# A fused transformer backward pass: kv and W' blocks between query halves, gate-gradient stores moved to GpSimd, two tails as column tiles

## The chip, the cores and the metric

The kernel runs on one core of a Trainium2 chip. The metric is the device time in microseconds of one execution, the median of several runs. A profile of one execution names its span, from the first instruction to the last. TensorE multiplies matrices out of SBUF into PSUM, VectorE (DVE), ScalarE (ACT) and GpSimd (POOL) work on elements, SyncE (SP) issues transfers; ScalarE and GpSimd issue some too. Each engine runs its own instructions in program order and waits on semaphores for the others.

## The reference

A block of a transformer, forward and backward: linear attention with 32 heads, then a gated MLP, each behind a layer norm and with a residual. Outputs are the block's result and the gradients of the input and of the five weight matrices. S = 2048 rows, D = 640, F = 1728, bf16.

```python
h  = x + A(layernorm(x));  h2 = h + B(layernorm(h))

def A(x):                       # wqkv: D x 3D, wo: D x D, 32 heads of 20
    q, k, v = heads(x @ wqkv)
    phi = lambda t: where(t > 0, t + 1, exp(t)) + 1e-6
    pq, pk = phi(q), phi(k)
    kv = einsum("bhsd,bhse->bhde", pk, v);  z = pk.sum over s
    o = (pq @ kv) / (pq . z + 1e-6)
    return o @ wo

def B(x):
    return (silu(x @ w1) * (x @ w3)) @ w2

out, vjp = jax.vjp(block, x, wqkv, wo, w1, w3, w2);  grads = vjp(grad_out)
```

## The kernel before, in words

Rows are worked in 16 tiles of 128 (`ST`), columns of D in five blocks of 128 (`DT`), the MLP in 14 chunks of 128 columns of F (`FT`; the last has only `FL` = 64) and four strips of 512 rows (`SC`). The order of the work is written out by hand: the Python program issues instructions one after another, and each engine's queue keeps that order. [...]named tiles rotate through a few buffers each, and a tile that is asked for again waits until the reader of its buffer's previous content is done.

The stages, with their times in the profile:

- 0 to 60 us: layer norm of x, the key projection with phi (`phi`, `phi_rest`), M = pk^T x (`m_part`, `m_end`), the sum z (`z_late`, `z_row`, which broadcasts it into `Zb`) and part of the query projection (`q_tile`). From 57 us on, `r_prod`, `r_red`, `r_inv`, `r_scale` make the normalised queries: a product with `Zb` on GpSimd, a sum per head, a reciprocal and a scaling on VectorE, and `r_T` transposes the result by DMA. `r_head(t)` is the last four of these for tile t.
- 60 to 90 us: the rest of M, the kv blocks (`kvT_block` and `f2_kv`, whose masked copy goes to `bd`), and W' = kv wo (`f2_wT`, which reads `bd` and is transposed into `Wp` by DMA). `q_late(t, between)` computes one query tile in two halves of 320 columns; `between` is put between the first and the second half. `run(...)` is the list in which all of these are put in order.
- 90 to 103 us: the attention output plus residual, tile by tile and half by half (`f2_half`, `f2_at`), its layer-norm statistics (`Stats.part`: VectorE, then a pow on GpSimd), the normalised `hn` (`f2_hn`) and its transpose by TensorE (`f2_ht` for the first four tiles). `mlp_ghh(n)` is chunk n of the MLP's upstream gradient g w2^T (`ghh_chunk`), some of which are computed here ahead of their use.
- 103 to 349 us: the MLP forward and the element-wise part of its backward, strip by strip and chunk by chunk (`mlp`, `mlp_pair`). `ghh` runs two chunks ahead. Two chunks make a pair; VectorE's seven products of a pair go out through `drain`, between other work. Results go to DRAM (`store`): `hh`, and the two halves of `gg_d`, the gate and the up gradients. `o2_steps` is the MLP's second product of the strip before, spread between chunks.
- 349 to 408 us: the w2 gradient (13 chunks of 128 rows of F, and a 64-row tail, `gw2_tail`).
- 408 to 571 us: the gradient of `hn`, the layer norm's backward, the attention's backward up to queries.
- 571 to 636 us: gradients of wqkv (`grad_halves`, called through `fill` as filler), the small D x D squares (`square`, `unload`: ScalarE copies 380 columns, then VectorE 260), transposes of `gkvT` (`trk`), and the key gradient per tile. The squares, `trk` and the key gradient share the three PSUM buffers `dkv`.
- 636 to 830 us: the gradient of x (`e_gxn`), then the gradients of w1 and w3 as 40 jobs of 432 columns (`grad_job`), each copied by ScalarE and stored.

The lines that the change moves most in `run` and in the MLP pair, before:

```python
(q_late, 10, f2_mT), (f2_kv, 2), (f2_kv, 3), (f2_kv, 4), (phi_rest,), (q_late, 11), (f2_wT, 0), (f2_wT, 1),
...
op(gate, gate, gh, to=gg_d, r0=F)          # store issued by SyncE
...
for i in range(DT):
    unload(square(wqT[:, 2 * DT:, :], gkvT, i), gm[:, i, :])
    if i > 0:
        fill(1)
```

Of the kernel before, what the change touches and what calls it, by code (L numbers as in the profile page):

```python
# [9 lines left out]
P = 128  # L10
# [45 lines left out]
def kernel(  # L56
# [73 lines left out]
    class Stats:  # L130
# [13 lines left out]
        def part(self, src, t, j):  # L144
            if j == 0:
                self.st[t] = cp.tile([P, 2, 6], F32, name="st6", bufs=4)
            V.bn_stats(out=self.st[t][:, j, :], in_=src[:, t, j * HD:(j + 1) * HD])
            if j == 0:
                return
            V.bn_aggr(out=self.mv[:, t, :], in_=self.st.pop(t)[:])  # L150
            V.tensor_scalar(out=self.ve[:, t:t + 1], in0=self.mv[:, t, 1:2], scalar1=EPS_LN, scalar2=None, op0=ALU.add)
            G.tensor_tensor(out=self.rs[:, t:t + 1], in0=self.ve[:, t:t + 1], in1=mhalf[:, 0:1], op=ALU.pow)

# [214 lines left out]
    def ghh_chunk(n, acc):  # L368

        c, fc = divmod(n, FT)  # L370
        mm5_to(acc, w2T, fc, g2T[c])
        if n % 2 == 0:
            ghh[n // 2] = pf.tile([P, 2, W], BF16, name="ghh", bufs=4)
        A.copy(out=ghh[n // 2][:, n % 2, :], in_=acc[:])  # L374
# [141 lines left out]
    m_part(2, range(8))  # L516
    z_row((0, 1), big())
    z_row((2, 3, 4), big())
# [3 lines left out]
    m_part(2, range(8, ST))  # L522
# [29 lines left out]
    r_head(5)  # L552
    r_prod(7)
# [167 lines left out]
    def mlp_pair(c, k, sig, s2, gate, up, gh):  # L721
# [14 lines left out]
        op(gate, gate, gh, to=gg_d, r0=F)  # L736
# [4 lines left out]
    def o2_steps(c, q=dma, tag="o2"):  # L741
# [4 lines left out]
        for n, (i, j, fc) in enumerate(jobs):  # L746
            if fc == 0:
                o2["ps"] = ps.tile([P, 512], F32, name="o2", tag=tag, bufs=2)
                if j == 0:
                    o2["sb"] = pf.tile([P, D], BF16, name="h2", bufs=2)  # L750
            T.matmul(o2["ps"][:, 0:HD], lhsT=hhT[c][:, fc, i * P:(i + 1) * P],  # L751
                     rhs=w2[:, fc, j * HD:(j + 1) * HD], start=(fc == 0), stop=(fc == FT - 1))
            if fc == FT - 1:
# [3 lines left out]
                if j == 1:  # L757
                    q(out=out0S[:, t, :], in_=o2["sb"][:])
# [17 lines left out]
    def run(*steps):  # L776
# [5 lines left out]
    run((q_late, 10, f2_mT), (f2_kv, 2), (f2_kv, 3), (f2_kv, 4), (phi_rest,), (q_late, 11), (f2_wT, 0), (f2_wT, 1),  # L782
        (phi_rest,), (q_late, 12), (f2_wT, 2), (f2_wT, 3), (phi_rest,), (q_late, 13, lambda: f2_wT(4)),
        (r_red, 6), (r_inv, 6), (r_scale, 6), (load_x, 2, 4), (r_T, 6), (q_late, 14), (load_x, 4, 8), (load_g2T, 1), (r_store, 4, 6),
        (mlp_ghh, 4), (q_late, 15),
        (sig_table,), (f2_half, 0, 0), (f2_half, 1, 0), (f2_half, 0, 1), (f2_half, 1, 1), (f2_hn, 0), (mlp_ghh, 5),
        (f2_half, 2, 0), (f2_hn, 1), (f2_m_out,), (load_w2T, 8 * P, 10 * P), (f2_half, 2, 1),
        (f2_ht, 0), (mlp_ghh, 6), (f2_half, 3, 0), (f2_hn, 2), (f2_w_out,), (f2_ht, 1), (f2_half, 3, 1), (phi_rest, 2),
        (q_out, 10, 14), (f2_ht, 2), (f2_hn, 3), (mlp_ghh, 7), (load_w2T, 10 * P, F), (f2_half, 4, 0), (f2_ht, 3),
        (f2_half, 4, 1), (r4_out,), (r_red, 7), (r_inv, 7), (r_scale, 7), (r_T, 7), (r_store, 6, 8), (q_out, 8, 10))  # L790
# [39 lines left out]
    for c in range(SC):  # L830
# [8 lines left out]
        for fc in range(FT):  # L839
# [17 lines left out]
            if fc == 3 and 0 < c < SC - 1:  # L857
# [59 lines left out]
    gt = ps.tile([P, DT, FL], F32, name="gt", tag="gw", bufs=4)  # L917

    def gw2_tail():

        for c in range(DT):
            for t in range(ST):
                T.matmul(gt[:, c, :], lhsT=g2[:, t, c * P:(c + 1) * P], rhs=hb[3][:, t, P:P + FL],  # L923
                         start=(c == 0 and t == 0), stop=(t == ST - 1), skip_group_check=True)
        sb = br.tile([P, DT, FL], BF16, name="gts")
        A.copy(out=sb[:], in_=gt[:])
        return sb

    def gw2_tail_out(sb):
        tr = ps.tile([P, DT, P], BF16, name="gttr", tag="gw", bufs=4)  # L930
        for c in range(DT):
            T.transpose(tr[:FL, c, :], sb[:, c, :], ident[:])
        ob = br.tile([P, D], BF16, name="gw2o", bufs=2)
        A.copy(out=ob[:FL].rearrange("p (c n) -> p c n", c=DT), in_=tr[:FL])
        A.dma_start(out=out_6[F - FL:F, :], in_=ob[:FL])

    for fc in range(FT - 1):
        b, i = divmod(fc, 4)
        if fc == FT - 2:
            sb = gw2_tail()  # L940
        acc = ps.tile([P, 2, 512], F32, name="gw", bufs=4)
        for j in range(2):
# [3 lines left out]
            if fc == FT - 2 and j == 0:  # L946
                gw2_tail_out(sb)
# [284 lines left out]

    fill(4)
# [8 lines left out]
    for i in range(DT):  # L1242
        unload(square(qp, kvN, i), dwoT[:, i, :])
        if i > 0:
            fill(1)
    dma(out=rows(dwoT_d), in_=dwoT[:])
    br.release()
# [7 lines left out]
    bo.release()  # L1255
    bv = pool("bv")
    pkT = bv.tile([P, DT, S], BF16, name="pkT")
    small = bv.tile([P, ST, D], BF16, name="small", tag="hnN")
    mN, gkv_b, gm = (small[:, n:n + DT] for n in (0, DT, 2 * DT))
    gzd = small[:, 3 * DT, :].rearrange("p (m q) -> p m q", q=P)  # L1260
# [4 lines left out]
    dma(out=mN, in_=m_v)  # L1265
# [3 lines left out]
    for i in range(DT):  # L1269
        unload(square(wqT[:, 2 * DT:, :], gkvT, i), gm[:, i, :])  # L1270
        if i > 0:
# [8 lines left out]
    for c, ms in SQ_BLOCKS:  # L1280
        tr = ps.tile([P, len(ms), P], BF16, name="trk", tag="dkv", bufs=3)
        for i, m in enumerate(ms):
            T.transpose(tr[:, i, :], gkvT[:, m, c * P:(c + 1) * P], ident[:])
        V.tensor_copy(out=gkv_b[:, c, ms[0] * P:(ms[-1] + 1) * P].rearrange("p (i q) -> p i q", q=P), in_=tr[:])

    for t in range(ST):
# [23 lines left out]
        if t == 1:  # L1310
            load_xnT(3)
        if t in (0, 4):
            load_wqT(t // 4)
# [110 lines left out]
```

## Time and profile before

| | |
|---|---|
| device time, median of 3 runs | 832.5 us (831.24 to 832.78) |
| span of the profiled execution | 830.0 us |
| TensorE busy | 818.9 us, 5540 matmuls |
| VectorE busy | 454.3 us |
| ScalarE busy | 319.4 us |
| GpSimd busy | 110.2 us |
| TensorE's share of the chain that ended last | 88% |
| moved by DMA | 157.59 MB, mean 190 GB/s |
| stores of `gg_d` from `gate` (SyncE) | 24 of 256 KB, median 3.4 us to landing |
| stores of `gg_d` from `ghh` (GpSimd) | 24 of 256 KB, median 3.4 us to landing |

Busy time is the time in which at least one instruction of the engine is in flight. Matmuls are pipelined, so a single one lasts longer than the distance to the next: what counts for TensorE is the distance from start to start. Idle time of an engine that is not the bottleneck costs nothing. The chain of waits follows the end of the kernel back through what released each step.

### The profile page before, as it was taken

Reading aid. Unit: us, or ns where it says so; the run is one execution under the profiler, and the core shown is the slowest. Engines: PE = TensorE matmul, PEld = TensorE weight load, DVE = VectorE, ACT = ScalarE, POOL = GpSimd, SP = SyncE. Lnnn points to the kernel's source line nnn. Section 1 sums busy time; section 2 is a strip of 40 time slices with the busy share of each in tenths; the row PEclk is TensorE's granted clock in tenths of the full one; section 3 lists DMA queues with packets and bytes.
Section 4 is the critical chain, followed back from the end, with each engine's and each line's share of the span. In section 5 each row is a group of like instructions: output and inputs, shape, how many; then the busy total and the mean of one; then the engine's idle time right before and its main releaser. Section 6 shows DMA issues by size and latency. Waiting matters only on the chain.

```text
span 830.0 us, 14209 instructions
## 1 busy us (share of the span) xinstructions
PE 818.9 (99%) x5540; PEld 523.8 (63%) x5568; DVE 454.3 (55%) x960; ACT 319.4 (38%) x605; POOL 110.2 (13%) x160
## 2 busy tenths in 40 slices
PE   8999999999999999999999999999999999999998
PEld 6676644555555555777777777777777777555554
DVE  7859787899898656400057777772681545200000
ACT  5855777655555666011121221222212433211111
POOL 2335222122121100000001111110220000000000
PEclk9999999999999999999999999999999999999999
DMA  9799998686474465999877888346997688886761
GB/s 259 207 322 182 218 305 248 220 214 170 139 203 144 127 205 166 211 248 268 229 151 187 183 214 207 66 104 112 228 265 150 157 193 180 209 197 135 168 164 37
DMA packets 323315, 157.59 MB, mean 190 GB/s; under 512 B 235312, under 2 KB 318160, under 8 KB 323248
## 3 DMA queue, kind: packets, MB, share of 16 engines
q1 hardware_dynamic: 293696, 127.73, 64.3%
q10 hardware_dynamic: 24416, 11.23, 6.4%
q0 software_dynamic: 5136, 17.73, 6.1%
q8 instruction: 43, 0.70, 0.4%
q14 instruction: 24, 0.20, 0.1%
HBM read 48.15 MB, written 51.46 MB: 120 GB/s over the span
## 4 chain that ended last, share of the span: by engine, by line
PE 88%; ACT 1%; DMA 1%; issue 0%; DVE 0%; ACTq 0%
PE mm L364 20%; PE job L1189 19%; PE ghn L991 14%; PE gxn L1348 8%; PE o L751 7%; PE gw L944 7%; PE gwo L1076 3%; PE dkv L1292 3%; PE gr L1048 3%; PE at L572 2%; PE mm L255 1%; PE dkv L1221 1%; DMA gg_d<-gate 1%; PE gt L923 0%; PE wt L610 0%
## 5 line engine op out<-in xcount | busy, mean ns | idle before, releaser
L1189 PE MATMUL job<-gb,hnN 128*128 128x432 bf16 x640 | 117.0, 346 | 0.0
L991 PEld LDWEIGHTS <-ggb 128*128 128x128 bf16 x864 | 84.5, 98 | 32.9
L1189 PEld LDWEIGHTS <-hnN 128*128 128x128 bf16 x640 | 62.6, 98 | 54.1
L364 PE MATMUL mm<-pqT,w 128*128 128x512 bf16 x398 | 93.1, 379 | 0.6
L364 PEld LDWEIGHTS <-w 128*128 128x128 bf16 x540 | 52.8, 98 | 63.4 <-issue 0.3
L1193 ACT CAST obs<-job 128x432 bf16<-128x432 f32 (+1 forms) x60 | 29.1, 485 | 123.1 <-PE job L1189 123.1
L751 PE MATMUL o<-w,hhT 128*128 128x320 bf16 x448 | 67.6, 299 | 0.1
L364 PE MATMUL mm<-g2T,w2T 128*128 128x512 bf16 x245 | 62.9, 379 | 1.1 <-ACT gate L693 0.5
L991 PE MATMUL ghn<-w13a,ggb 128*128 128x320 bf16 x448 | 63.5, 299 | 0.0
L991 PE MATMUL ghn<-w13b,ggb 128*128 128x320 bf16 x416 | 61.4, 299 | 0.0
L751 PEld LDWEIGHTS <-hhT 128*128 128x128 bf16 x448 | 43.8, 98 | 23.6
L944 PE MATMUL gw<-g,hb 128*128 128x320 bf16 x416 | 57.0, 299 | 0.0
L374 ACT CAST ghh<-mm 128x512 bf16<-128x512 f32 x52 | 30.5, 587 | 55.0 <-PE mm L364 50.1
L944 PEld LDWEIGHTS <-hb 128*128 128x128 bf16 x416 | 40.5, 98 | 15.8
L1348 PE MATMUL gxn<-wqT,gT 128*128 128x320 bf16 x320 | 48.7, 299 | 0.0
L1056 POOL TENSOR_TENSOR sz<-Zb,g_h 128x640 f32<-128x640 bf16 x16 | 20.2, 1261 | 199.4 <-DVE g_h L1054 107.7
L364 PEld LDWEIGHTS <-w2T 128*128 128x128 bf16 x280 | 27.2, 98 | 27.4 <-issue 2.4
L691 ACT ACTIVATE sig<-mm 128x512 bf16<-128x512 f32 x56 | 33.5, 599 | 28.4 <-PE mm L364 24.9
L1003 ACT ACTIVATE gs<-ghn 128x640 bf16<-128x640 f32 x16 | 11.2, 703 | 78.6 <-PE ghn L991 73.7
L255 PE MATMUL big<-wqkv,pqT 128*128 128x320 bf16 x260 | 39.3, 300 | 1.1 <-ACT pqT L251 0.6
L255 PEld LDWEIGHTS <-pqT 128*128 128x128 bf16 x320 | 30.5, 98 | 14.3 <-ACT pqT L251 2.2
L1348 PEld LDWEIGHTS <-gT 128*128 128x128 bf16 x320 | 31.3, 98 | 12.2
(196 smaller groups left out, 1253.4 us busy)
## 6 DMA issues: line engine op xcount, KB each, us to landing
hh_d<-hhT SPq DMA_DIRECT2D x24, 256.0 KB, 2.6
gg_d<-gate SPq DMA_DIRECT2D x24, 256.0 KB, 3.4
gg_d<-ghh POOLq DMA_DIRECT2D x24, 256.0 KB, 3.4
ggb<-gg_d SPq DMA_DIRECT2D x6, 896.0 KB, 6.5
ggb<-gg_d SPq DMA_DIRECT2D x6, 832.0 KB, 7.2
out_dram<-obs ACTq DMA_DIRECT2D x40, 108.0 KB, 2.7
x_sb<-in_A_x_dram SPq DMA_DIRECT2D x6, 640.0 KB, 6.1
ggb<-gg_d SPq DMA_DIRECT2D x2, 1728.0 KB, 12.8
```

What stands on the lines that cost most here:

```text
L255: T.matmul(acc, lhsT=pqT[:, c, t * P:(t + 1) * P], rhs=wqkv[:, c, n0:n0 + HD], start=(c == 0), stop=(c == DT - 1))
L364: T.matmul(acc[:], lhsT=w[:, c, fc * P:(fc + 1) * P], rhs=rhs[:, c, :], start=(c == 0), stop=(c == DT - 1))
L374: A.copy(out=ghh[n // 2][:, n % 2, :], in_=acc[:])
L691: A.activation(sig[:, i, :], gp[:], AF.Sigmoid)
L751: T.matmul(o2["ps"][:, 0:HD], lhsT=hhT[c][:, fc, i * P:(i + 1) * P], rhs=w2[:, fc, j * HD:(j + 1) * HD], start=(fc == 0), stop=(fc == FT - 1))
L944: T.matmul(acc[:, j, 0:HD], lhsT=hb[b][:, t, i * P:(i + 1) * P], rhs=g2[:, t, j * HD:(j + 1) * HD], start=(t == 0), stop=(t == ST - 1))
L991: T.matmul(acc[:, j, 0:HD], lhsT=ggb[t // 2][:, k, lo:lo + P], rhs=rhs[:, j * HD:(j + 1) * HD], start=(k == 0), stop=(k == NG - 1))
L1048: T.matmul(gr[t][:, j, 0:HD], lhsT=ghT[t][:, c, :], rhs=wT2[:, c, j * HD:(j + 1) * HD], start=(c == 0), stop=(c == DT - 1))
L1076: T.matmul(acc[m][:, j, 0:n], lhsT=r_sb[:, t, m * P:(m + 1) * P], rhs=g_hx[:, t, j * HD:j * HD + n], start=(t == 0), stop=(t == ST - 1))
L1189: T.matmul(acc[:, 0:n], lhsT=lhs[:, t, m * P:(m + 1) * P], rhs=rhs(t), start=(t == 0), stop=(t == ST - 1))
L1193: A.copy(out=ob, in_=acc[:, 0:n])
L1348: T.matmul(acc[:, j, 0:HD], lhsT=g, rhs=wqT[:, k, j * HD:(j + 1) * HD], start=(k == 0), stop=(k == 14))
```

## The change

Seven groups of edits. They reorder work around gaps of TensorE, let transfers start elsewhere, and shorten products that use half of the array.

1. `z_row`'s two products go into one two-bank buffer, two tiles of M later.
2. The three kv blocks stand between the halves of query tile 11, the W' blocks in pairs between the halves of tiles 12 and 13, the last in tile 14. `r_head(5)` and `r_prod(7)` move from before the end of M to after that. In the following section `ghh` chunks, loads and stores are in another order, and the transposed load of the second strip of `grad_out` moves into the MLP.
3. The gate gradient is stored by GpSimd.
4. The last `ghh` chunk of a strip (64 columns of F) and the tail of the w2 gradient become pairs of products on 64 columns of the array each: their outputs lie in PSUM partitions 0 to 63 and 64 to 127, one for each half of the moving columns.
5. The last strip's MLP output is written over `x_sb` and stored from there.
6. In the backward pass, `xnT(3)`, `wqT(0)` and `mN` are loaded earlier, and the transposes `trk` stand between the squares.
7. The last of the 40 jobs is cut into 304 and 128 columns.

(`Stats.part` gains an argument, and a method `center` is added; nothing calls them.)

```diff
     def ghh_chunk(n, acc):
         c, fc = divmod(n, FT)
+        if fc == FT - 1:
+            gh, hw = ghh[n // 2], W // 2
+            G.memset(gh[FL:, 1, :], 0.0)
+            for d in range(DT):
+                for h in range(2):
+                    T.matmul(acc[h * FL:(h + 1) * FL, 0:hw], lhsT=w2T[:, d, fc * P:fc * P + FL],
+                             rhs=g2T[c][:, d, h * hw:(h + 1) * hw], start=(d == 0), stop=(d == DT - 1))
+            for h in range(2):
+                A.copy(out=gh[:FL, 1, h * hw:(h + 1) * hw], in_=acc[h * FL:(h + 1) * FL, 0:hw])
+            return
         mm5_to(acc, w2T, fc, g2T[c])
...
     z_late((2, 3, 4), big())
-    m_part(2, range(8))
-    z_row((0, 1), big())
-    z_row((2, 3, 4), big())
+    m_part(2, range(10))
+    zr = ps.tile([P, 2, 512], F32, name="bigx", tag="big", bufs=2)
+    z_row((0, 1), zr[:, 0])
+    z_row((2, 3, 4), zr[:, 1])
     r_prod(0)
     q_tile(5)
     r_prod(1)
-    m_part(2, range(8, ST))
+    m_part(2, range(10, ST))
...
     m_part(4, range(5, 11))
     q_tile(9)
-    r_head(5)
-    r_prod(7)
     phi_rest()
...
-        op(gate, gate, gh, to=gg_d, r0=F)
+        op(gate, gate, gh, to=gg_d, r0=F, q=dmaG)
...
                 if j == 0:
-                    o2["sb"] = pf.tile([P, D], BF16, name="h2", bufs=2)
+                    t = c * TPC + i
+                    o2["sb"] = x_sb[:, t, :] if c == SC - 1 else pf.tile([P, D], BF16, name="h2", bufs=2)[:]
...
-    run((q_late, 10, f2_mT), (f2_kv, 2), (f2_kv, 3), (f2_kv, 4), (phi_rest,), (q_late, 11), (f2_wT, 0), (f2_wT, 1),
-        (phi_rest,), (q_late, 12), (f2_wT, 2), (f2_wT, 3), (phi_rest,), (q_late, 13, lambda: f2_wT(4)),
-        (r_red, 6), (r_inv, 6), (r_scale, 6), (load_x, 2, 4), (r_T, 6), (q_late, 14), (load_x, 4, 8), (load_g2T, 1), (r_store, 4, 6),
-        (mlp_ghh, 4), (q_late, 15),
-        (sig_table,), (f2_half, 0, 0), (f2_half, 1, 0), (f2_half, 0, 1), (f2_half, 1, 1), (f2_hn, 0), (mlp_ghh, 5),
-        (f2_half, 2, 0), (f2_hn, 1), (f2_m_out,), (load_w2T, 8 * P, 10 * P), (f2_half, 2, 1),
-        (f2_ht, 0), (mlp_ghh, 6), (f2_half, 3, 0), (f2_hn, 2), (f2_w_out,), (f2_ht, 1), (f2_half, 3, 1), (phi_rest, 2),
-        (q_out, 10, 14), (f2_ht, 2), (f2_hn, 3), (mlp_ghh, 7), (load_w2T, 10 * P, F), (f2_half, 4, 0), (f2_ht, 3),
-        (f2_half, 4, 1), (r4_out,), (r_red, 7), (r_inv, 7), (r_scale, 7), (r_T, 7), (r_store, 6, 8), (q_out, 8, 10))
+    def kv3():
+        for m in (2, 3, 4):
+            f2_kv(m)
+
+    run((q_late, 10, f2_mT), (q_late, 11, kv3), (phi_rest,), (r_store, 4, 5),
+        (q_late, 12, lambda: (f2_wT(0), f2_wT(1))), (q_late, 13, lambda: (f2_wT(2), f2_wT(3))), (phi_rest,),
+        (q_late, 14, lambda: f2_wT(4)), (load_x, 2, 4), (r_head, 5), (r_prod, 7), (r_red, 6), (r_inv, 6), (f2_m_out,), (f2_w_out,),
+        (load_x, 4, 8), (q_out, 10, 14), (r_store, 5, 6), (load_w2T, 8 * P, 10 * P), (mlp_ghh, 4), (q_late, 15),
+        (sig_table,), (f2_half, 0, 0), (f2_half, 1, 0), (mlp_ghh, 5), (f2_half, 0, 1), (f2_half, 1, 1), (f2_hn, 0),
+        (f2_half, 2, 0), (f2_hn, 1), (load_w2T, 10 * P, F), (f2_half, 2, 1),
+        (f2_ht, 0), (f2_half, 3, 0), (f2_hn, 2), (f2_half, 3, 1), (mlp_ghh, 6), (f2_ht, 1), (mlp_ghh, 7), (f2_ht, 2),
+        (f2_hn, 3), (f2_half, 4, 0), (f2_ht, 3), (f2_half, 4, 1), (r_scale, 6), (r_T, 6), (r_red, 7), (r_inv, 7),
+        (r_scale, 7), (r_T, 7), (r4_out,), (r_store, 6, 8), (q_out, 8, 10))
...
-            if fc == 3 and 0 < c < SC - 1:
+            if fc == (6, 3, 3)[min(c, 2)] and c < SC - 1:
                 load_g2T(c + 1)
...
     def gw2_tail():
-        for c in range(DT):
-            for t in range(ST):
-                T.matmul(gt[:, c, :], lhsT=g2[:, t, c * P:(c + 1) * P], rhs=hb[3][:, t, P:P + FL],
-                         start=(c == 0 and t == 0), stop=(t == ST - 1), skip_group_check=True)
...
-    def gw2_tail_out(sb):
...
+        gt = ps.tile([P, 2, 512], F32, name="gt", tag="gw", bufs=4)
+        for t in range(ST):
+            for j in range(2):
+                T.matmul(gt[j * FL:(j + 1) * FL, 0, 0:HD], lhsT=hb[3][:, t, P:P + FL],
+                         rhs=g2[:, t, j * HD:(j + 1) * HD], start=(t == 0), stop=(t == ST - 1))
+        ob = br.tile([P, HD], BF16, name="gts")
+        A.copy(out=ob[:], in_=gt[:, 0, 0:HD])
+        for j in range(2):
+            A.dma_start(out=out_6[F - FL:F, j * HD:(j + 1) * HD], in_=ob[j * FL:(j + 1) * FL, :])
...
+    load_xnT(3)
+    load_wqT(0)
     fill(4)
...
+    dma(out=mN, in_=m_v)
+    dma(out=rows(dwoT_d), in_=dwoT[:])
...
-    for i in range(DT):
+    for i, (c, ms) in enumerate(SQ_BLOCKS):
         unload(square(wqT[:, 2 * DT:, :], gkvT, i), gm[:, i, :])
+        tr = ps.tile([P, len(ms), P], BF16, name="trk", tag="dkv", bufs=3)
+        for k, m in enumerate(ms):
+            T.transpose(tr[:, k, :], gkvT[:, m, c * P:(c + 1) * P], ident[:])
+        V.tensor_copy(out=gkv_b[:, c, ms[0] * P:(ms[-1] + 1) * P].rearrange("p (i q) -> p i q", q=P), in_=tr[:])
         if i > 0:
             fill(1)
...
-    for c, ms in SQ_BLOCKS:
-        tr = ps.tile([P, len(ms), P], BF16, name="trk", tag="dkv", bufs=3)
...
-        if t == 1:
-            load_xnT(3)
-        if t in (0, 4):
-            load_wqT(t // 4)
+        if t == 2:
+            load_wqT(1)
...
-            grad_job(hnN, m, lambda t: gb[i][:, t, :], NB, out[:, m, f0:f0 + NB], A.dma_start)
+            last = (i, m) == (len(blocks) - 1, DT - 1)
+            for a, b in ((0, NB - P), (NB - P, NB)) if last else ((0, NB),):
+                grad_job(hnN, m, lambda t: gb[i][:, t, a:b], b - a, out[:, m, f0 + a:f0 + b], A.dma_start)
```

## The prediction

> **What bounds the kernel now.** I read the engine table first, then the chain of waits, then the waits of TensorE by releaser, then the timeline around each gap.
>
> ```profile
> PE 818.9 (99%) x5540; PEld 523.8 (63%) x5568; DVE 454.3 (55%) x960; ACT 319.4 (38%) x605; POOL 110.2 (13%) x160
> ```
>
> TensorE has an instruction in flight in 99% of the span, which doesn't yet say that it runs at its rate. The chain of waits (start, us, what) gives the rate:
>
> ```profile
> 348.76 52.16 PE gw L944 x384
> 401.20 2.33 PE gt L923 x80
> 403.53 2.17 PE gw L944 x16
> 406.10 2.28 PE gw L944 x16
> 709.69 116.81 PE job L1189 x640
> ```
>
> 116.81/640 = 182.5 ns for 432 columns and 52.16/384 = 135.8 ns for 320: 0.417 ns a column plus 2.4 ns. The 64-column tail product fits: 2.33/80 = 29.1 ns. So 512 columns cost 215.8, 256 cost 109.2, 128 cost 55.8. Everywhere after 120 us the starts follow this rule, except around 405 us and 589 us. The kernel is TensorE's own columns, and a change pays only where it removes columns or one of the few gaps. The waits of TensorE in the whole span (total, times, longest):
>
> ```profile
> PE wt L610 <- DVE bd L205: 0.7, 1, 0.7
> PE kv L404 <- DMA mT<-mbs: 0.6, 1, 0.6
> PE mm L364 <- ACT gate L693: 0.5, 1, 0.5
> PE trh L663 <- DVE hn L155: 0.4, 1, 0.4
> PE big L255 <- ACT Zb L324: 0.3, 1, 0.3
> PE trk L1283 <- DVE small L1284: 0.2, 1, 0.2
> ```
>
> These count from the end of the instruction before, with its tail of some 0.17 us. From start to start by the rule above, the losses that the change can reach are: 0.46 at 57 us (Zb), 0.78 at 78 (mT), 0.83 at 81 (bd), 0.13 at 91, 0.53, 0.20 and 0.26 at 99 to 103 (hn and the copy of its transpose), 0.48 at 117 (gate), 0.19 at 405, 0.38 + 0.23 + 0.10 at 589, 0.19 at 595. Together 4.8 us, 0.6% of the span.
>
> Three of them need the timeline. First, VectorE before the kv blocks:
>
> ```profile
> 77.93 0.87 DVE L343 TENSOR_REDUCE rden<-pr 128x16 f32<-128x320 f32 x2
> 79.74 0.97 DVE L350 TENSOR_TENSOR pql<-pql,rden 128x640 bf16<-128x640 bf16 x1
> 81.46 0.74 DVE L205 TENSOR_TENSOR bd<-kv,mask 128x160 bf16<-128x160 f32 x3
> ```
>
> The first two belong to `r_head(5)`; the mask that W' waits for stands behind them. Then the store of the gate gradient:
>
> ```profile
> 109.08 2.68 SPq L354 DMA_TRANSPOSE pqT<-pql  x1
> 110.37 0.68 DVE L727 TENSOR_TENSOR gate<-gate,ghh 128x1024 bf16<-128x1024 bf16 x1
> 113.00 0.41 SPq L710 DMA_DIRECT2D gg_d<-gate  x1
> 117.57 0.58 ACT L693 CAST gate<-mm 128x512 bf16<-128x512 f32 x1 [1.91 <-DMA gg_d<-gate]
> ```
>
> The product is there at 111.05; SyncE is busy with a transpose and two stores until 113.00, and ScalarE gets the buffer back only at 117.5. Last, the switch to a 64-column stationary operand:
>
> ```profile
> 405.00 0.71 PE L944 MATMUL gw<-g,hb 128*128 128x320 bf16 x4
> 405.63 0.47 PE L932 MATMUL gttr<-ident,gts 128*64 128x128 bf16 x5
> 406.03 0.58 PE L944 MATMUL gw<-g,hb 128*128 128x320 bf16 x3
> ```
>
> Four matmuls from 405.00 would hand over at 405.54 and five transposes from 405.63 at 405.91 to 405.94; it was 405.63 and 406.03. So about 0.09 us is lost on the way in and again on the way out.
>
> **What the Trainium skill says.** "TensorEngine Tiling (Array Packing)", Key Properties: column tiles compute independently, and a change of tiling mode drains the engine. The 0.09 us above agree with the drain; no two tiles run side by side in this trace. "TensorE: Matmul & The Clock Gate", Measured speedup vs the span model: three column tiles gave 2.38x, about 4 ns more per tile. That is not shown here. The same page, Weight-path perf modes, has the fast weight load on only for 128 weights; the five 64-wide loads at 405.6 us take 109 ns against 98, and the transposes behind them still start 56 ns apart, so I expect loads to stay hidden.
>
> **The change part by part.**
>
> *Column tiles.* The last chunk of `ghh` in each of four strips: before 5 x 215.8 = 1.08 us. After, ten matmuls of 256 columns in two column groups: side by side 5 x (109.2 + 4) + 2 x 0.09 = 0.75, in series 10 x 109.2 + 0.18 = 1.27. Four strips: -1.3 us or +0.8. The tail of the w2 gradient: before 2.33 + 5 x 0.056 + 0.19 = 2.80. After, 32 of 320 columns: paired 16 x 139.8 + 0.18 = 2.42 (-0.4), in series 4.53 (+1.7). I take side by side; that is the largest unknown, 2.1 + 2.1 = 4.2 us between its ends. The second 256-wide ScalarE copy and the GpSimd memset are hidden: ScalarE is busy 10 to 13 of each 20 us there, GpSimd 4.
>
> *57 us.* One `zr` buffer lets `q_tile(5)` take the buffer of `z_late`, free long before: -0.46. Zb comes two tiles (0.54 us) later, which only GpSimd's `r_prod` feels.
>
> *kv and W'.* kv moves behind another half product, 5 x 0.136 = 0.68. mT was awaited until 78.69; SyncE issues transposes back to back from 66.4 us up to it, so it follows only in part when TensorE arrives earlier. I keep 0.3 of the 0.78. For W', `r_head(5)` (2.4 us of VectorE) leaves; the mask is done about 0.5 us after the kv blocks, W' asks 1.36 us after: -0.83. Sum with 57 us: -1.8.
>
> *The W'x section, 88 to 103 us.* The 2.4 us of `r_head(5)` and 1.4 of `r_red(6)`, `r_inv(6)` now stand before the first VectorE add of `f2_half(0, 0)`, at about 90.7, where TensorE could be served at 89.3. From there VectorE sets the pace: add 0.49, statistics 0.49, norm 0.44 and small ones come to about 10 us until hn(3). `ghh(5)` moved ahead covers Wp, but no longer lies between hn(0) and `f2_ht(0)`: only 2.3 us of TensorE work stand there against a chain of 2.8 (92.45 to 95.24 in the trace). I expect 0.5 to 0.8 lost at ht(0), 0.4 at ht(3), so 0.5 of the 1.8 is given back: -1.3 (range -0.4 to -2.2).
>
> *117 us.* Issued by GpSimd at about 111.1 in place of 113.0, with 0.74 us of issue in place of 0.41 (the ghh stores' time there), the first gate store should land 1.5 us sooner; ScalarE needed 0.5 us of wait to go away: -0.4. Behind the store on GpSimd wait the pow steps of ln2, whose inputs come later in VectorE's order anyway; 24 issues of 0.74 us are 18 us spread over 230. `g2T` loads at strip 0, chunk 6 instead of at 93 us: needed some 18 us later.
>
> *589 us.* Transposes between the squares take away the 0.71 at 589 us, and an earlier load of mN the 0.19 before its first square at 595.66. But `dkv` has three buffers: square 0, trk 0, square 1, and then trk 1 wants the buffer of square 0 with no filler between. Its copies come after five `gzd` (to 583.47), then VectorE's 583.69 to 584.12; TensorE is there at 583.38. That is a new stall of 0.8. Net -0.1 (range -0.6 to +0.3).
>
> *The end.* The last copy has 128 columns instead of 432: at (0.52 - 0.42)/112 = 0.9 ns a column, -0.27, and 0.04 for one more split: -0.2. `o2` into `x_sb`, the stores of `r`, `w2T` in another order: beside TensorE's columns, 0.
>
> Sum: -1.3 - 0.4 - 1.3 - 0.4 - 0.1 - 0.2 = -3.7; 832.5 - 3.7 = 828.8.
>
> **The rivals.** (A) Column tiles in series: +0.8 + 1.7 and the rest at -2.0: 833.0, no change or slightly slower. For it: nothing in this trace shows two tiles at once. Against: the measured factor of the skill. (B) The gaps stay gone: no stall at ht(0) or trk 1: -1.3 - 0.4 - 2.2 - 0.4 - 0.7 - 0.2 = -5.2, 827.3. For it: VectorE is busy 15.8 of 20 us from 80 to 100, so not full; against: the counts above. (C) VectorE's moved work costs more than it freed, or the gate stores crowd GpSimd where VectorE is busy 19.2 of 20 us (strip 1): the gains from 57 to 117 us vanish, and if VectorE stood still for each of strip 1's seven issues, 7 x 0.74 less the 4% of 40 us that it has idle there = 3.6 us come on top: 832.5 - 1.7 - 0.3 + 3.6 = 834.1. For it: that 96%. Against: the ghh stores go through GpSimd already and VectorE's product beside one took 0.69 as elsewhere.
>
> **How the numbers follow.** Forecast 55% (827.9 to 830.5), A 18%, B 17%, C 10%. Range 826.7 to 833.3: it takes in most of A and B and leaves out C and the far end of B. Faster by over 0.2% (below 830.8): the forecast, B, and a little of A: 0.72. Within 0.2%: most of A and the tail of the forecast: 0.16. Slower: C and the rest of A: 0.12.
>
> **What would show it.** The ten ghh matmuls of the last chunk should start in pairs about 4 ns apart, a pair 113 ns; starts 109 apart mean A. W' without a wait on bd; kv waiting 0.1 to 0.5 on mT; trh at ht(0) waiting on hn; trk 1 waiting 0.8 on VectorE's copy; no wait of ScalarE's gate copy on its store. A VectorE wait on GpSimd in strip 1 would make it C.

## The result and the profile after

| | before | after |
|---|---|---|
| device time, median | 832.64 us (831.24 to 834.79, 4 runs) | 828.02 us (827.15 to 829.11, 4 runs) |
| ratio to before | | 0.9943, 95% interval 0.9918 to 0.9968 |
| timed a second time | 831.8 us (830.93 to 833.37, 12 runs) | 829.17 us (827.46 to 830.61, 7 runs), ratio 0.9963 (0.9950 to 0.9976) |
| span of the profiled execution | 830.0 us | 826.7 us |

The change makes the kernel 0.4 to 0.6% faster. The two timings of the changed kernel differ by 1.15 us in the median, and its single runs lie up to 3.5 us apart. One source of that, seen in the traces, is among the findings below.

The engine table of the page, after:

```profile
PE 817.6 (99%) x5551; PEld 523.6 (63%) x5551; DVE 453.7 (55%) x960; ACT 319.0 (39%) x609; POOL 134.3 (16%) x196
```

TensorE is still busy in 99% of the span and has 1.3 us less of busy time; GpSimd has 24 us more, of which 21 are its 32 issues of gate stores (24 of 256 KB and eight smaller ones): `gate_sp` below, which takes them back, has 112.9 us. The number of matmuls hasn't grown: before, 5540 records stand against 5568 weight loads, so 28 matmul records are missing from that trace; now both are 5551. The waits of TensorE by releaser (total, times, longest) are the counterpart of those shown of before:

```profile
PE mm L369 <- ACT gate L707: 0.6, 1, 0.6
PE trk L1284 <- DVE small L1236: 0.6, 1, 0.6
...
PE bigx L327 <- ACT Zb L329: 0.5, 1, 0.5
...
PE trh L677 <- DVE hn L160: 0.4, 1, 0.4
```

The waits on `mT` and `bd` have left the list. The wait of `trh` is there as before, that on the gate copy too, and two are new: the second `z_row` product on ScalarE's copy of the first, and `trk` on VectorE.

The span by stages, each from the first start of one product to the first start of the next, in the two profiled executions ("the squares" begin with the products into `gkvT` and end at the first product with `xnT`):

| stage (us) | before | after | difference | the prediction's terms |
|---|---|---|---|---|
| start to first z product | 57.07 | 57.70 | +0.63 | two M tiles moved ahead of it, 0.54 |
| to the first MLP product | 45.92 | 43.64 | -2.28, or -1.74 without those tiles | -1.3 |
| strip 0 of the MLP, to the first `o2` product | 46.54 | 46.55 | 0.0 | -0.3 (one chunk) - 0.4 (gate) |
| strips 1 to 3, to the w2 gradient | 199.07 | 198.14 | -0.93 | -1.0 (three chunks) |
| w2 gradient | 59.62 | 59.19 | -0.43 | -0.4 |
| to the squares | 166.83 | 166.83 | 0.0 | 0 |
| squares and `trk` | 15.28 | 15.36 | +0.08 | the -0.1 of 589 us is for this row and a part of the next |
| to the end of TensorE's work | 236.18 | 236.02 | -0.16 | mN's wait gone |
| last copy and store | 3.49 | 3.26 | -0.23 | -0.2 |
| sum | 829.99 | 826.68 | -3.31 | -3.7 |

### The profile page after: what moved, and what is told of

Its sections match the earlier page's. It is cut to its first block, busy times and chain, and to the rows that moved or that the text cites. A ratio compares the mean times of both kernels' runs of the same rounds, so it can differ in the third digit from the quotient of the medians.

```text
span 826.7 us, 14217 instructions
## 1 busy us (share of the span) xinstructions
PE 817.6 (99%) x5551; PEld 523.6 (63%) x5551; DVE 453.7 (55%) x960; ACT 319.0 (39%) x609; POOL 134.3 (16%) x196
## 4 chain that ended last, share of the span: by engine, by line
PE 94%; ACT 2%; DVE 2%; DMA 1%; issue 1%; SPq 0%; DVEq 0%; ACTq 0%; POOLq 0%
PE mm L369 19%; PE job L1198 19%; PE ghn L1000 14%; PE gxn L1356 8%; PE o L766 7%; PE gw L955 7%; PE big L260 4%; PE gwo L1085 3%; PE gr L1057 3%; PE dkv L1302 3%; PE macc L400 3%; PE at L586 2%; DMA wqkv<-in_A_wqkv_dram 1%; PE dkv L1230 1%; DMA gg_d<-gate 1%
## 5 line engine op out<-in xcount | busy, mean ns | idle before, releaser
L1198 PE MATMUL job<-gb,hnN 128*128 128x432 bf16 (+2 forms) x656 | 117.0, 342 | 0.0
L1202 ACT CAST obs<-job 128x432 bf16<-128x432 f32 (+3 forms) x61 | 29.3, 481 | 123.0 <-PE job L1198 123.0
L369 PE MATMUL mm<-g2T,w2T 128*128 128x512 bf16 x240 | 59.6, 379 | 0.6 <-ACT gate L707 0.6
L389 ACT CAST ghh<-mm 128x512 bf16<-128x512 f32 x48 | 28.2, 588 | 46.3 <-PE mm L369 40.6
L369 PEld LDWEIGHTS <-w2T 128*128 128x128 bf16 x260 | 25.3, 98 | 25.8 <-issue 2.6
```

Of the source, the lines that this page charges most:

```text
L369: T.matmul(acc[:], lhsT=w[:, c, fc * P:(fc + 1) * P], rhs=rhs[:, c, :], start=(c == 0), stop=(c == DT - 1))
L1198: T.matmul(acc[:, 0:n], lhsT=lhs[:, t, m * P:(m + 1) * P], rhs=rhs(t), start=(t == 0), stop=(t == ST - 1))
L1202: A.copy(out=ob, in_=acc[:, 0:n])
```

## The experiments

Where an experiment has no repetition, it is one profiled execution; "lost" is time from start to start beyond 0.417 ns a column plus 2.5 ns. The first z product came at 57.3 to 59.9 us in the executions of the changed kernel and its variants, so stages are compared, not ends.

**1. Do two column tiles run side by side, and does it depend on the order?** In the changed kernel the ten matmuls of a last `ghh` chunk alternate between the tiles. The view of this one line in the first strip of the changed kernel (durations min/median/max, first and last start):

```profile
L381 PEld LDWEIGHTS <-w2T x10: 106/110/110, 136.4 to 136.8; 128*64 128x64 bf16 x10
L381 PE MATMUL mm<-g2T,w2T x10: 272/273/297, 136.4 to 136.9; 128*64 128x256 bf16 x10
```

Ten matmuls of 256 columns, 273 ns each, start within 0.46 us: in series that would be 9 x 109 = 0.98. Their starts in the trace (us):

```
136.412 .415 | .545 .549 | .654 .658 | .764 .767 | .873 .876
```

Pairs 3 to 4 ns apart, the second pair 133 ns after the first and the others every 109 to 110 ns. The other three strips show the same. `h_outer` puts the loop over tiles outside:

```diff
-            for d in range(DT):
-                for h in range(2):
+            for h in range(2):
+                for d in range(DT):
```

> The changed kernel with the ten matmuls of the last ghh chunk in another order: five on the first column group, then five on the second, in place of alternating. Same instructions, same loads. Theory (two column groups stream side by side only if neighbours in the queue differ in their group): a chunk goes from 0.74 us to 9 x 109.3 ns and one overlap plus 0.19 = 1.17 us, four chunks +1.7 us at the end. Rival (a product on 64 columns is cheaper by itself, whatever stands beside it): a chunk stays at 0.74 us and the end does not move.

Measured: 827.88 us, span 826.2. The view of the line:

```profile
L381 PE MATMUL mm<-g2T,w2T x10: 272/273/297, 135.4 to 136.0; 128*64 128x256 bf16 x10
```

The starts are 135.358, .491, .497, .600, .630, .709, .739, .818, .848, .958. A tile can't start two products 6 ns apart when each takes 107 ns of columns, so these are two streams (.358, .491, .600, .709, .818 and .497, .630, .739, .848, .958), 139 ns apart. The trace doesn't name the tile of a product, but the two matmuls at .358 and .497 last 297 ns and the other eight 272 or 273, as the first of each tile does in the alternating order. All five of the first tile come first in the Python program; the second tile's first nevertheless starts before the first tile's third. So, as far as the starts show it, products of different column tiles don't keep program order between them. From what is before it to what follows the chunk costs 0.90 us, 0.14 more than the 0.76 of alternating: neither 1.17 nor 0.74.

**2. What are the tiles worth to the whole?** `full_ghh` takes the tiles out of `ghh_chunk` again and leaves those of the w2 gradient.

```diff
-        if fc == FT - 1:
-            gh, hw = ghh[n // 2], W // 2
...
-            return
         mm5_to(acc, w2T, fc, g2T[c])
```

> The changed kernel with the last ghh chunk of each strip computed as before (five matmuls of 512 columns over the padded 128 rows); the w2-gradient tail keeps its column tiles. Theory (the column tiles are worth the time that their starts show, 0.31 us a chunk, and nothing fills it otherwise): each of the four chunks takes 1.08 us again, TensorE reaches the w2 gradient 1.2 us later than in the changed kernel (347.3 in place of 346.0), the span is 1.2 us longer (827.9). Rival (TensorE's time in the MLP strips is set by others, so the shorter chunk only moves a wait): the w2 gradient starts within 0.4 us of the changed kernel's.

Measured: strips 1 to 3 take 199.11 us against 198.14, +0.97 or 0.32 a chunk, and nothing filled that time otherwise: the theory holds for the chunks. The span was 830.4 us, 3.7 more, which the chunks don't explain: 2.04 us were lost in strip 0 (experiment 6), and 0.47 and 0.61 in waits on transfers at 576 and 694 us and 0.26 at 703 us that other executions don't have.

**3. The z products.** At 57 us the timeline of the changed kernel has (start, us, engine, line, operation, in brackets the idle time before and what ended it):

```profile
57.70 0.27 PE L327 MATMUL bigx<-dz,ones 128*128 128x128 bf16 x2
58.01 0.37 ACT L329 CAST Zb<-bigx 128x256 bf16<-128x256 f32 x1 [2.64 <-PE bigx L327]
58.43 0.33 PE L327 MATMUL bigx<-dz,ones 128*128 128x128 bf16 x3 [0.46 <-ACT Zb L329]
```

The third to fifth product write the second bank of `zr`, the copy reads the first, and still they wait until it has ended at 58.38: `zr` is the only tile that the copy and these products share. From start to start 0.62 us are lost, where before 0.46 were. `z_both` issues both groups of products ahead of both copies:

```diff
-    z_row((0, 1), zr[:, 0])
-    z_row((2, 3, 4), zr[:, 1])
+    for go in (z_row((0, 1), zr[:, 0]), z_row((2, 3, 4), zr[:, 1])):
+        go()
```

> The changed kernel, but both products of z into zr are issued before either of the two copies to Zb. Theory (the second product waits for the copy of the first because both lie in one tile): the wait of 0.6 us at 58 us goes; as mT then lands later than TensorE asks, 0.1 to 0.4 of it comes back as a wait of kv at 78 us, and the MLP starts 0.2 to 0.5 us earlier than 101.33. Rival 1 (the second product waits for dz or for nothing that moves): the wait stays. Rival 2 (the chain of transposes sets 78 us anyway): the wait goes and all of it comes back at kv, MLP start at 101.3.

Measured: 826.93 us, span 825.2. The wait on `Zb` is gone from the list, the stage from the z product to the MLP takes 42.96 us in place of 43.64, and nothing was given back to a wait on `mT` in this execution. In experiment 9, with the same edit, `kv` lost 0.73 us on `mT`, which is more than the edit saves. So the repair is real, but whether it stays depends on when the transpose lands.

**4. `trk` behind the following square.** In the lines below, `trk(...)` stands for the transposes of one group and their copy, which the changed kernel writes out in place.

```diff
     for i in range(DT):
         unload(square(wqT[:, 2 * DT:, :], gkvT, i), gm[:, i, :])
-        trk(*SQ_BLOCKS[i])
         if i > 0:
+            trk(*SQ_BLOCKS[i - 1])
             fill(1)
+        if i == DT - 1:
+            trk(*SQ_BLOCKS[i])
```

The place in the changed kernel:

```profile
579.57 0.90 DVE L1278 TENSOR_SCALAR small<-ident,gz 128x128 bf16<-128x128 bf16 x5
...
580.05 0.49 PE L1230 MATMUL dkv<-bd,wqT 128*128 128x140 bf16 x6
...
580.69 0.43 DVE L1236 CAST small<-dkv 128x260 bf16<-128x260 f32 x1 [0.22 <-ACT small L1236]
581.03 0.28 DVE L1285 COPY small<-trk 128x256 bf16<-128x256 bf16 x1
581.17 0.33 PE L1284 MATMUL trk<-ident,bd 128*128 128x128 bf16 x3 [0.63 <-DVE small L1236]
```

The second `trk` wants the buffer of square 0. VectorE's part of that copy starts 0.22 us after the five `gzd` products, when ScalarE's part has ended, and ends itself at 581.12.

> The changed kernel with each group of transposes one square later: square 0, square 1, trk 0, filler, square 2, trk 1, and so on. Theory (trk 1 waits for the buffer of square 0): the stall of 0.79 us at 580 us is gone and no other takes its place, so the gradient of x starts 0.7 to 0.8 us earlier in relation to the start of the gkvT products. Rival (VectorE's copies set the pace of this stretch): the stall moves to a later trk or to the first key-gradient tile, 0 to 0.3 us gained.

Measured: 827.15 us, span 825.4. The stage of the squares takes 14.57 us in place of 15.36, -0.79, and no other wait took its place there (a wait of 0.57 us on a transfer at 502 us, which the edit doesn't touch, stands in this trace alone).

**5. The W'x section.** `ht_late` changes one place in the list:

```diff
-        (f2_ht, 0), (f2_half, 3, 0), (f2_hn, 2), (f2_half, 3, 1), ...
+        (f2_half, 3, 0), (f2_ht, 0), (f2_hn, 2), (f2_half, 3, 1), ...
```

> The changed kernel with f2_ht(0), the transposes of the first hn tile, behind f2_half(3, 0) in place of ahead of it. Theory (VectorE's chain of adds, statistics and norms sets the pace of the W'x section, as my prediction counted): the 0.52 us stall at the first trh goes, but hn(3) isn't ready sooner, so TensorE waits 0.5 us longer at the last trh, and the MLP starts within 0.15 us of the changed kernel's 101.3 us (taken from its z_row start). Rival (the stall is a local one, with slack behind it): the MLP starts 0.4 to 0.55 us sooner.

Measured: the loss at the first `trh` (0.52) is gone and that at the last grew from 0.15 to 0.68; from `kv` to the first MLP product it takes 22.44 us against 22.43. VectorE's chain sets the pace there: a stall filled at one place came back at the next.

`head5_back` puts `r_head(5)` and `r_prod(7)` back behind `q_tile(9)`.

```diff
     q_tile(9)
+    r_head(5)
+    r_prod(7)
     phi_rest()
...
-        (load_x, 2, 4), (r_head, 5), (r_prod, 7), (r_red, 6), ...
+        (load_x, 2, 4), (r_red, 6), ...
```

> The changed kernel with r_head(5) and r_prod(7) back at their old place before the end of the M products. Theory (it is the 2.4 us of VectorE's work in r_head(5) that held the masks bd back, and so W'): with kv in the new place the mask waits for VectorE, W' starts 0.5 to 0.9 us later after kv than in the changed kernel (kv to W' 2.8 to 3.2 us in place of 2.31), and the 0.52 us stall at ht(0) shrinks by 0.3 to 0.5 since r_head(5) no longer stands before the adds of the halves; the MLP starts 0 to 0.5 us later. Rival (placing kv and W' between the query halves was enough): kv to W' stays at 2.3 us, the stall at ht(0) goes, and the MLP starts 0.5 us sooner.

Measured: span 834.7 us. The waits of TensorE:

```profile
PE at L588 <- DMA Wp<-pkx: 6.2, 1, 6.2
PE wt L626 <- DVE bd L210: 1.2, 1, 1.2
```

From `kv` to W' it takes 3.68 us in place of 2.31: the theory's cause is right, its size (0.5 to 0.9) too small. What neither expected is the 6.2 us. W' comes 1.4 us later, so its transposes do, and the stores that the change has put behind them on another queue no longer stand behind them:

```profile
88.54 0.88 POOL L633 DMA_DIRECT2D wT_d<-pkx  x1 [7.00 <-DVE rden L348]
```

In the trace of this kernel the last of five W' transposes is issued at 90.42 and lands at 99.00, 8.6 us later; in the changed kernel it is issued at 87.83, ahead of the same store at 89.36, and lands after 2.6. That the stores hold it back is read from this order in one execution and wasn't tested by itself. From the z product to the MLP it takes 53.1 us in place of 43.6; a part of that is TensorE's own rate, since from 99 to 103 us it ran at half rate after the long wait (see the last section).

**6. What the wait at 116 us hangs on.** The chain in the changed kernel, from its timeline:

```profile
102.27 0.49 DVE L591 TENSOR_TENSOR x_sb<-at,x_sb 128x320 bf16<-128x320 f32 x1 [2.23 <-DMA x_sb<-in_A_x_dram]
...
110.31 0.68 DVE L741 TENSOR_TENSOR gate<-gate,ghh 128x1024 bf16<-128x1024 bf16 x1
...
111.60 0.73 POOL L724 DMA_DIRECT2D gg_d<-gate  x1 [1.61 <-ACT s L706]
...
116.24 0.59 ACT L707 CAST gate<-mm 128x512 bf16<-128x512 f32 x1 [1.77 <-DMA gg_d<-gate]
116.87 1.24 PE L369 MATMUL mm<-g2T,w2T 128*128 128x512 bf16 x5 [0.63 <-ACT gate L707]
```

VectorE's add waits for a load of x tiles 4 to 7; the gate products stand behind it on VectorE, the store behind them, ScalarE's buffer behind the store, TensorE's PSUM buffer behind ScalarE. That load was issued at 92.71 and landed at 102.17, 9.5 us later, behind stores issued from 88.8 to 91.0 us; in the kernel before, where those stores come at 96 to 107 us, it took 5.1 us. Two experiments on it:

`gate_sp` gives the gate store back to SyncE.

```diff
-        op(gate, gate, gh, to=gg_d, r0=F, q=dmaG)
+        op(gate, gate, gh, to=gg_d, r0=F)
```

> The changed kernel with the store of the gate product issued by SyncE again. Theory (the store by GpSimd buys little, because its landing is set by the transfers that crowd the DMA engines from 89 to 100 us and later, not by its issue): the span is within 0.6 us of the changed kernel's, and any difference stands at one place, the ScalarE gate copy of strip 0, where TensorE waits 0.5 to 1.0 us at 116 us; the later strips show no wait of ScalarE's gate copy on the store longer than 0.3 us. Rival (my prediction's step: an issue by GpSimd is 1.5 us sooner in every strip): the wait at 116 us is 0.5 to 1 us longer than in the changed kernel, and other strips show waits of TensorE on the gate copy too, 0.5 us a strip, 2 us in all.

`x_early` moves the load ahead of the stores:

```diff
-        (q_late, 14, ...), (load_x, 2, 4), (r_head, 5), ..., (f2_w_out,), (load_x, 4, 8), (q_out, 10, 14), ...
+        (q_late, 14, ...), (load_x, 2, 4), (load_x, 4, 8), (r_head, 5), ..., (f2_w_out,), (q_out, 10, 14), ...
```

> The changed kernel with the load of x tiles 4 to 7 issued right behind that of tiles 2 and 3, ahead of the transpose that waits for r_head(5). Theory (VectorE's add of tile 4 waits 2.2 us for this load, its products of strip 0 run late, and so the first gate store): VectorE's wait at 102 us is gone, the gate store is issued 1 to 1.5 us earlier in relation to the MLP start, TensorE's wait of 0.6 us at 116 us is gone; end -0.4 to -0.6 us. Rival (the transfers between 89 and 100 us are at their limit, and the store through GpSimd is slow by itself): the add no longer waits, but another transfer does, or the gate store lands as late as before; end -0.2 to +0.3 us.

Measured, with every traced kernel that has this part of the order unchanged beside them:

| traced kernel | VectorE's wait for the load (us) | gate store landed, us after the first MLP product | TensorE lost, 103 to 120 us |
|---|---|---|---|
| `h_outer`, `ht_late`, `trk_behind`, `after_again` (the changed kernel again) | 0.83, 0.84, 0.90, 1.00 | 13.50, 13.60, 13.50, 13.87 | 0 |
| `z_both` | 1.44 | 14.00 | 0.14 |
| `gate_sp` (store by SyncE) | 1.82 | 14.25 | 0.39 |
| the changed kernel | 2.23 | 14.83 | 0.97 |
| `full_ghh` | 3.34 | 15.90 | 2.04 |
| `z_trk_both` | 3.51 | 16.55 | 2.70 |
| `x_early` (load moved) | none | 14.38 | 0.52 |

The loss follows the landing of one load, 0 to 2.7 us with the same code around it. In all nine traces in which VectorE waits for it, the gate product ends 7.44 us plus that wait after the first MLP product. And in every row TensorE's loss is the time by which the gate store lands later than 13.86 us, to within 0.01. The kernel before fits too, with a landing at 14.51 and a loss of 0.64. The issuing engine is a separate matter:

```profile
111.19 0.69 DVE L741 TENSOR_TENSOR gate<-gate,ghh 128x1024 bf16<-128x1024 bf16 x1
...
111.95 1.16 SPq L724 DMA_DIRECT2D gg_d<-gate  x1
```

In `gate_sp` SyncE issues this store 0.07 us after the product's end; it no longer stands behind a transpose, as it did in the kernel before. In the changed kernel GpSimd issues it 0.60 us after (110.99 to 111.60), and in each of the 28 pairs of chunks the delay is 0.55 to 0.60 us; SyncE's delay in `gate_sp` is 0.06 us in the median of the 28 and 4.6 at most. So the issue by GpSimd is steady, but it gained nothing here, and in the later strips TensorE loses nothing on a gate copy in either kernel. In the changed kernel's own second trace nothing was lost at all. `x_early` shows the other half. The load still took 10.1 us (issued 89.73, landed 99.85), VectorE no longer waited for it, and yet the gate store took 5.7 us to land and TensorE lost 0.52: the transfers behind were later instead. From 90 to 120 us the stretches of the changed kernel's timeline give the 16 DMA engines a mean busy share of 1.03 to 1.09: they are full. Why the same load lands after 8.2 us in one execution and after 10.8 in another isn't settled.

**7. Later stores.** `stores_late` moves `f2_m_out`, `f2_w_out`, `q_out(10, 14)` and `r_store(5, 6)` from ahead of the section to behind `(f2_half, 3, 1)`.

```diff
-        ..., (r_inv, 6), (f2_m_out,), (f2_w_out,), (load_x, 4, 8), (q_out, 10, 14), (r_store, 5, 6), (load_w2T, 8 * P, 10 * P), ...
+        ..., (r_inv, 6), (load_x, 4, 8), (load_w2T, 8 * P, 10 * P), ...
-        ..., (f2_half, 3, 1), (mlp_ghh, 6), ...
+        ..., (f2_half, 3, 1), (f2_m_out,), (f2_w_out,), (q_out, 10, 14), (r_store, 5, 6), (mlp_ghh, 6), ...
```

> The changed kernel with four groups of stores (m, W', q tiles 10 to 14, r tile 5) moved from 89 to 92 us to behind the last W'x product of the third pair, about 97 us. Theory (these stores crowd the DMA engines, which holds back the load of x tiles 4 to 7, VectorE's add, its product and with it the gate store): load_x(4, 8) lands in 5 to 6 us after its issue in place of 9.5, VectorE's wait at add 4 (2.2 us) is below 0.5, the gate store is issued near 110 us, and TensorE's wait at 116 us is below 0.15; the MLP's first strip ends 0.4 to 0.6 us sooner. Rival (the crowd only moves to 97 to 107 us, where the gate store and the loads of g2T stand): the load lands sooner, but the gate store takes over 5 us to land and TensorE still waits 0.3 to 0.6 us at 116 us.

Measured: span 832.4 us. The load landed in 5.5 us, as the theory has it, and VectorE's wait for it was gone. But the stores then met the MLP's:

```profile
113.34 0.73 POOL L724 DMA_DIRECT2D gg_d<-gate  x1 [2.80 <-ACT gate L707]
...
120.28 0.58 ACT L707 CAST gate<-mm 128x512 bf16<-128x512 f32 x1 [3.52 <-DMA gg_d<-gate]
...
120.92 1.35 PE L369 MATMUL mm<-g2T,w2T 128*128 128x512 bf16 x4 [2.38 <-ACT gate L707]
```

The gate store took 6.9 us, TensorE lost 2.5 us, and then ran slowly for 3.4 us. The stage of strip 0 is 3.3 us longer than in the changed kernel. The rival is right, and the early place that the change gives these stores is worth keeping.

**8. An earlier load.** `x_first` is the kernel of experiment 9 with the load of x tiles 4 to 7 moved to right behind that of tiles 0 and 1, at 79 us.

```diff
     load_x(0, 2)
+    load_x(4, 8)
...
-        (load_x, 4, 8), (q_out, 10, 14), ...
+        (q_out, 10, 14), ...
```

> The kernel with both repairs (z products and trk), and in it the load of x tiles 4 to 7 moved from about 93 us to right behind the load of tiles 0 and 1 at 79 us, where the DMA engines are 0.6 busy. Theory (that load is the head of a chain in the first strip: load, VectorE's add of x tile 4, the gate product behind it, the gate store, ScalarE's buffer, TensorE; and its spread from execution to execution is a part of the time's spread): VectorE's add of tile 4 waits for no load, the gate store is issued at 109 to 110 us, TensorE loses under 0.5 us in all between 106 and 118 us in place of 0 to 2.7, the median is 0.3 to 1.2 us under that of both repairs alone (827.18), a ratio of 0.991 to 0.993 to the kernel before. Rival 1 (the load runs beside the transposes of W' at 82 to 90 us, which TensorE needs at once): TensorE waits 0.5 to 3 us for Wp near 88 us and the time is the same or higher. Rival 2 (the stores that follow keep the DMA engines full up to 120 us whatever comes first): the gate store still takes over 5 us, TensorE still waits 0.5 us at 116 us, the median is within 0.3 us of 827.18.

Measured: 832.36 us median (827.17 to 835.2, 22 runs), ratio 0.9996 (0.9980 to 1.0011): all of the gain is gone. Seven runs lie from 827.2 to 829.2 and fifteen from 831.6 to 835.2, with nothing between. The traced one is of the fifteen; its waits of TensorE:

```profile
PE at L585 <- DMA x_sb<-in_A_x_dram: 3.5, 1, 3.5
PE at L587 <- DMA Wp<-pkx: 1.6, 1, 1.6
```

Rival 1 is right. The DMA engines' busy share from 80 to 90 us is 1.03 (0.61 in the changed kernel), the last W' transpose lands in 4.7 us in place of 2.6, and the load of tiles 2 and 3 in 9.3 in place of 3.6, although it is issued right behind the store of W' in both kernels. That load's wait of 3.5 us, the longer of the two, wasn't expected by any of the three. The mean granted clock of each run separates the two groups: 0.999 or 1.000 in the seven, 0.996 or 0.998 in the fifteen. The traced run, at 0.998, has one stretch of 3.4 us at half rate behind the wait of 3.5 us, so the longer runs seem to pay for a wait and for the rate after it (see the last section). Why some executions get the long wait isn't shown, since none of the seven was traced.

**9. Both repairs** (`z_trk_both`: experiments 3 and 4 together), timed beside the changed kernel.

> The changed kernel with both repairs: the two z products ahead of the two copies of Zb, and each set of trk transposes behind the following square. Theory (the two stalls of 0.62 and 0.79 us are on TensorE's path and nothing takes their place): 1.4 to 1.7 us under the changed kernel timed beside it, 826.4 to 826.7 where that one is at 828.0, 0.9925 of the kernel before. Rival (waits on transfers in other places of the span differ by more from execution to execution and take it up): within 0.5 us of the changed kernel.

> The changed kernel once more, timed beside the kernel with both repairs: 828.0 plus or minus 1.0 us, a ratio of 0.9935 to 0.9955 to the kernel before.

Measured: 827.18 us (825.64 to 829.97, 6 runs), ratio to before 0.9935 (0.9922 to 0.9948), against 829.17 and 0.9963 (0.9950 to 0.9976) for the changed kernel: 2.0 us less in the medians, a little over the 1.4 to 1.7 expected, so it is faster than the changed kernel and the kernel before. Its traced run was the slowest of the six, and shows why a single trace can't rank such versions:

```profile
104.17 0.49 DVE L591 TENSOR_TENSOR x_sb<-at,x_sb 128x320 bf16<-128x320 f32 x1 [3.51 <-DMA x_sb<-in_A_x_dram]
...
107.78 0.59 ACT L713 CAST up<-mm 128x512 bf16<-128x512 f32 x1 [2.99 <-POOL ln_rs L154]
...
118.58 0.59 ACT L707 CAST gate<-mm 128x512 bf16<-128x512 f32 x1 [2.21 <-DMA gg_d<-gate]
```

What the repairs bring (here only the 0.79 of `trk`, since kv waits 0.73 us for `mT` again) is outweighed by 2.7 us behind one late load. The changed kernel itself came out at 829.17, just outside the 828.0 plus or minus 1.0 that was expected of it.

## Why the prediction was right or wrong, point by point

The forecast of -3.7 us lies between the two timings, -4.6 and -2.6, and near the profile's -3.3. Its terms, in its order:

- *Column tiles* (-1.3 and -0.4): right, and for the reason given. Pairs start 3 to 4 ns apart; a chunk takes 0.76 us where 0.75 was counted, the tail 2.39 where 2.42 was. The Trainium skill, "TensorE: Matmul & The Clock Gate", Measured speedup vs the span model, gives about 4 ns more a tile: this trace agrees, with 3 to 4 ns. At the change of mode 93 ns are lost on the way in and 96 on the way out, the 0.09 twice that was taken from before. Rival A is out. `full_ghh` shows that the time was free for the taking.
- *57 us* (-0.46): this step failed. "One `zr` buffer lets `q_tile(5)` take the buffer of `z_late`" is so, and the wait of `q_tile(5)` is gone. But I looked only at the buffer that came free and not at the new one's two readers and writers: the second group of products waits for the copy of the first, 0.62 us, so the term is +0.17. `z_both` removes it and with it 0.68 us of the stage.
- *kv and W'* (-0.5 and -0.83): W' exact, 3.14 us from kv to W' before and 2.31 after. Of kv's wait 0.06 is left in place of the 0.3 kept, in this execution; 0.34 in `ht_late` and 0.73 in `z_trk_both` show that the transposes do set it at times, as the step says. `head5_back` confirms that VectorE's `r_head(5)` was the cause of the wait on `bd`.
- *The W'x section* (0.5 given back): the places and the reason are right (`ht_late`), the stall at ht(0) is 0.52 of the 0.5 to 0.8 forecast, at ht(3) 0.15 in place of 0.4. But the same section had lost 0.53, 0.20 and 0.13 us before: the 0.9 to 1.2 that the step forecasts, less this 0.86, would have been 0.0 to 0.3 given back and not 0.5. It now loses 0.67, and nothing was given back. This error and that of 57 us (0.69 and 0.63) cancel almost wholly, by luck. The whole stage is -1.74 without the moved tiles, in place of -1.3, because kv's wait fell by 0.72 and not 0.5, and 0.13 before the second W' product went too.
- *117 us* (-0.4): not obtained in the profiled run, where strip 0 lost 0.97 us, obtained in the second trace, where it lost none. The size is misread at the outset: 0.48 is the idle time from the modelled end of the product before, and from start to start the loss in the kernel before was 0.64. The cause read for that kernel holds: the product was there at 111.05 and SyncE issued its store at 113.00. What failed is the step from there to the changed kernel. There the product itself ends 9.66 us after the first MLP product in place of 8.06, behind an add that waits 2.23 us for a load, and `gate_sp` shows SyncE issuing the store half a microsecond sooner behind its product than GpSimd does. The term that is mis-sized is the one put at nothing, "the stores of `r`, `w2T` in another order: beside TensorE's columns, 0": with the stores of m, W' and q early as well, the load behind them costs 0 to 2.7 us, from one execution to the next.
- *589 us* (-0.1): right to the size. The new stall of 0.8 stands where it was put, 0.79, and `trk_behind` takes it away. VectorE's copy waits there for ScalarE's part of the same square, which the step didn't name; in the trace of the kernel before, the 0.22 us between the last `gzd` and that copy (583.47 to 583.69) are the same wait.
- *The end* (-0.2): -0.23.

Rival B, all gaps gone, didn't come: the stalls at ht(0) and at the second `trk`, which it denies, are both in the trace, 0.52 and 0.79 us. Rival C didn't come either: in strip 1 VectorE is busy 38.73 of 40 us, before 38.72, beside GpSimd's 11.40 us in place of 8.12.

## What to carry to other kernels

List for every new buffer who writes and who reads each part of it, and whether the reader of one part stands ahead of the writer of the other: a wait can follow the tile and not the bank. Where the DMA engines are full, moving a transfer is a trade between its neighbours: moved later, the stores held back the MLP; moved earlier, a load held back W'; ask first in which stretch the engines have room and who waits for what is queued there. And judge an edit of half a microsecond by its own stage in the trace, since one late load elsewhere moved whole runs by more than that.

## What the runs showed of the hardware that was not expected

Products on two column tiles overlap even when the program has all of one tile's first, and start out of program order (experiment 1). This is an exception to the statement at the beginning that each engine runs its instructions in program order. The Trainium skill, "TensorE: Matmul & The Clock Gate", The mechanism, says of packed tiles that matmuls start and end strictly in program order; for two column tiles with five products each the measured starts differ, and the measurement decides. What is inferred here is only from the starts and durations, and takes the program's order to be that of the Python source, since the trace doesn't name the tile of a product.

TensorE can drop to half rate after a wait of only some 2 us. In `stores_late`, by stretches of the timeline (us, busy and count, granted clock, share of the DMA engines, GB/s):

```profile
110.00:118.00 8.00, 8.00 (x43) 1.00 1.05 266
118.00:121.00 3.00, 0.62 (x4) 1.00 1.15 210
121.00:125.00 4.00, 4.00 (x12) 0.57 1.10 364
125.00:130.00 5.00, 5.00 (x29) 1.00 0.91 192
```

After a wait of 2.4 us the products of 512 columns start 426 ns apart for about 3.4 us, in place of 216, which adds 1.7 us to the 2.5 lost. The Trainium skill, "TensorE: Matmul & The Clock Gate", What's actually happening, names an idle window of about 3.4 us for the drop to half; here a shorter wait sufficed. The length alone doesn't decide it. Of the losses of 2.1 to 2.5 us, two in `stores_late` (2.1 at 15 us and this one) were followed by half rate, and one each in `z_trk_both` (2.1 at 15 us) and `gate_sp` (2.4 at 16 us) were not, nor were any of those below 2 us. The losses of 3.7 us in `x_first` and 6.4 us in `head5_back` were followed by it. Where it came, it cost 1.7 to 2.1 us more than the wait.
